# Groups of Q, K, V columns 512, 512, 352 and 352 wide in place of four of 432

## The chip, the cores and the metric

One core of a Trainium2 chip runs the program. The metric is the device time of one execution in microseconds (us). Three runs of the kernel before took 1100.6, 1100.63 and 1102.8 us; their median, 1100.63, is the time before.

The engines are TensorE (PE, with its weight loads PEld), VectorE (DVE), ScalarE (ACT), GpSimd (POOL) and SyncE (SP). DMAs are issued by SP, ACT and POOL. In a profile, ACTq and SPq are the sequencers of ACT and SP, on which a DMA issue or a wait takes time.

## The reference

One transformer block for 2048 tokens of 576 values, all float32: sliding attention (32 heads of 18, a window of 8 tokens at distance 2) and an FFN with squared relu run side by side on the same normalised input.

```python
xn = _layernorm(x, axis=-1)                      # S=2048, D=576
return x + _A_ref(xn, A_wqkv, A_wo) + _B_ref(xn, B_w1, B_b1, B_w2, B_b2)
...
qkv = (x @ wqkv).reshape(B, S, 3, H, Dh)         # H=32, Dh=18
idx = pos[:, None] - off[None, :]                # off = 0, 2, ..., 14
logits = einsum("bhsd,bhswd->bhsw", q, kg) * scale
attn = softmax(where(mask, logits, -1e9))
o = einsum("bhsw,bhswd->bhsd", attn, vg) @ wo
...
h = x @ w1 + b1                                  # F=4608
h = where(h > 0, h, 0) ** 2
out = h @ w2 + b2
```

## The kernel before, in words

**Tiles.** The tokens form four blocks of 512, each of four rows of 128 tokens. The 576 inputs are five chunks of 128 (the last holds the 64 left over, doubled). Every float32 operand is split into a high and a low part that TensorE takes: ACT copies the high part, DVE subtracts for the low one. A product is high·high, low·high and high·low, so a row of 128 tokens times one group of columns is 14 matmuls (`row_products`, L342).

**Groups.** The 32 heads form four groups of eight, 144 columns of each of Q, K and V. A group's K, V and Q columns lie side by side, 432 in all, and one matmul is 432 wide: one PSUM bank holds 512.

**Where these products are.** Group 0 of block 0 runs first, in the open rows (L1391 on, matmuls at L1472). Then come the plain rows of blocks 0 and 1 (`qkv_row`, L366): groups 1, 3, 2 of block 0, and 3, 2, 1, 0 of block 1, four rows each, in five PSUM banks by turns; the last two rows lie inside the first pair of FFN tiles. Blocks 2 and 3 are done later, two groups (0 and 1, then 2 and 3) and two blocks at a time, by a scheme with seven products in place of eight (`quad_step`, L1091, products at L1103 and L1107); its last two steps lie inside the second FFN phase.

**What follows a row.** ACT copies the PSUM bank into a staging slot (L358; in the quads L1113, where DVE may add a second bank) and one DMA writes the three 144-column parts to a scratch tensor in DRAM, `kvq[g]` (L360, L1117). ACT issues that DMA for plain rows; in the quads ACT, SP, or, for the last ones, GpSimd. Attention on DVE later loads K and V of a whole block with the tokens before it (1.3 MB each, L388) and Q (L386). `offer` puts an attention on the list once its group and block are stored.

**What sets the order.** The instructions of each engine are written out in order by hand, and each engine runs its own list strictly in that order. Every DMA of SP and ACT reports to one of eight counters (DMAHW0 to DMAHW7), handed out in turn over both engines in the order of the program; a DMA is issued only when the one eight earlier, the last on its counter, has landed, and its engine waits for that.

**What the steps touch.** L590 is an ACT copy to a high part for the left-over inputs, followed by DVE's subtraction at L118 (the helper `tt`, so all of DVE's subtractions bear L118). L323 and the next L118 split a group's weights. L515 and L118 split the first FFN weights into the slot `w1s`, which the FFN's first product reads (L677). L743 and L746 are the start of an FFN pair's second sum: one matmul, and ACT's copy of its bank into another, to which the product after it adds. L524 reloads split FFN weights, 1 MB each. L573 is the FFN's second matmul.

## Time and profile before

| | before |
|---|---|
| median of the runs | 1100.63 us |
| span of the profiled execution | 1098.5 us (its time is taken as the median's, 2.1 us more) |
| TensorE busy | 1092.3 us, 99% |
| VectorE busy | 879.9 us, 80% |
| ScalarE busy | 563.2 us, 51% |
| DMA moved | 298.97 MB, 272 GB/s on average |
| granted TensorE clock | 9 of tenths or more in all 40 slices |

Rows of the profile read as follows. A row of the timeline is start, length, engine, line, operation, what it writes <- what it reads, the shape, how many of them (x12), and in brackets the idle time of the engine before it, with what it is taken to have waited for. A row with three numbers behind the name of an operation gives the shortest, median and longest of its durations in ns. "DMA to landing" is the time from a DMA's issue to its last byte, again shortest, median and longest, in us. A row that begins with a window gives the busy time and the number of instructions of PE, PEld, DVE, ACT and POOL, then the granted clock, the DMA share and GB/s.

### The profile page before, as it was taken

Reading aid. Unit: us, or ns where it says so; the run is one execution under the profiler, and the core shown is the slowest. Engines: PE = TensorE matmul, PEld = TensorE weight load, DVE = VectorE, ACT = ScalarE, POOL = GpSimd, SP = SyncE. Lnnn points to the kernel's source line nnn. Section 1 sums busy time; section 2 is a strip of 40 time slices with the busy share of each in tenths; the row PEclk is TensorE's granted clock in tenths of the full one; section 3 lists DMA queues with packets and bytes.
Section 4 is the critical chain, followed back from the end, with each engine's and each line's share of the span. In section 5 each row is a group of like instructions: output and inputs, shape, how many; then the busy total and the mean of one; then the engine's idle time right before and its main releaser. Section 6 shows DMA issues by size and latency. Waiting matters only on the chain.

```text
span 1098.5 us, 13947 instructions
## 1 busy us (share of the span) xinstructions
PE 1092.3 (99%) x4936; PEld 922.9 (84%) x4936; DVE 879.9 (80%) x1183; ACT 563.2 (51%) x794; POOL 149.3 (14%) x267
## 2 busy tenths in 40 slices
PE   9999999999999999999999999999999999999998
PEld 7999888888888888888899988888888888888887
DVE  7687988899898979999879387776767676889955
ACT  5435666656666654555344345454554545543432
POOL 4000401031030101003010300201101010101010
PEclk9999999999999999999999999999999999999999
DMA  8966998879989887868565988868686877685582
GB/s 282 340 221 214 342 391 314 338 268 257 393 317 294 317 332 261 306 225 315 197 211 168 320 318 284 305 224 315 222 294 221 294 241 288 224 284 194 185 290 83
DMA packets 109558, 298.97 MB, mean 272 GB/s; under 512 B 12648, under 2 KB 42736, under 8 KB 98608
## 3 DMA queue, kind: packets, MB, share of 16 engines
q1 hardware_dynamic: 69984, 192.84, 50.1%
q0 software_dynamic: 13200, 62.52, 16.2%
q10 hardware_dynamic: 26304, 42.71, 11.7%
q8 instruction: 39, 0.64, 0.2%
q14 instruction: 31, 0.25, 0.1%
HBM read 213.53 MB, written 84.50 MB: 271 GB/s over the span
## 4 chain that ended last, share of the span: by engine, by line
PE 99%; DVE 0%; ACT 0%; issue 0%; POOL 0%; ACTq 0%; POOLq 0%
PE p L573 47%; PE p L677 35%; PE p L366 7%; PE p L1103 6%; PE p L1107 1%; PE p L1472 1%; PE p L683 1%; PE p L1389 0%; PE p L1434 0%; DVE w1s L118 0%; ACT X L122 0%; PE p L1371 0%; ACT h L723 0%; DVE w2s L118 0%; DVE r L118 0%
## 5 line engine op out<-in xcount | busy, mean ns | idle before, releaser
L573 PE MATMUL p<-h,w2s 128*128 128x512 f32 x2066 | 491.6, 389 | 0.2 <-ACT h L723 0.2
L573 PEld LDWEIGHTS p<-h,w2s 128*128 128x128 f32 x2066 | 387.5, 188 | 81.7 <-ACT h L723 0.6
L677 PE MATMUL p<-X,w1s 128*128 128x512 f32 x864 | 219.2, 389 | 0.0
L677 PEld LDWEIGHTS p<-X,w1s 128*128 128x128 f32 x864 | 162.2, 188 | 33.5
L546 ACT ACTIVATE w2s<-w2r 128x640 fp32r<-128x640 f32 x164 | 120.3, 735 | 128.1 <-PE p L573 98.3
L118 DVE TENSOR_TENSOR w2s<-w2r,w2s 128x576 fp32r<-128x576 f32 x164 | 123.5, 753 | 72.3 <-ACT w2s L546 70.7
L677 PE MATMUL p<-S,w1s 128*128 128x512 f32 x648 | 164.5, 389 | 0.0
L677 PEld LDWEIGHTS p<-S,w1s 128*128 128x128 f32 x648 | 121.6, 188 | 25.1
L444 POOL DMA_DIRECT2D o<-q x128 | 69.5, 609 | 418.2 <-DVE q L118 416.7
L719 ACT ACTIVATE r<-r,b1t 128x512 f32<-128x512 f32 x72 | 52.2, 725 | 116.8 <-DVE r L118 115.7
L415 DVE TENSOR_REDUCE lg<-pr 128x64 f32<-128x1152 f32 x64 | 86.5, 1351 | 1.2
L118 DVE TENSOR_TENSOR pr<-lg,kv 128x1152 f32<-128x1152 f32 x64 | 86.6, 1354 | 1.0
L118 DVE TENSOR_TENSOR pr<-q,kv 128x1152 f32<-128x1152 f32 x64 | 86.6, 1354 | 0.9
L118 DVE TENSOR_TENSOR pr<-pr 128x576 f32<-128x576 f32 (+1 forms) x128 | 77.6, 606 | 3.5
L118 DVE TENSOR_TENSOR r<-p,r 128x512 f32<-128x512 f32 (+1 forms) x77 | 53.1, 689 | 32.8 <-ACT r L785 15.3
L727 ACT ACTIVATE r<-r 128x1024 f32<-128x1024 f32 x72 | 76.1, 1056 | 1.2
L118 DVE TENSOR_TENSOR h<-r,h 128x1024 fp32r<-128x1024 f32 (+3 forms) x46 | 51.8, 1135 | 23.4 <-ACT r L727 14.9
L761 ACT ACTIVATE r<-p 128x512 f32<-128x512 f32 x36 | 21.5, 598 | 82.1 <-PE p L677 82.1
L118 DVE TENSOR_TENSOR w1s<-w1r,w1s 128x1024 fp32r<-128x1024 f32 (+2 forms) x42 | 46.2, 1103 | 9.5 <-ACT w1s L515 8.8
L719 ACT ACTIVATE r<-p,b1t 128x512 f32<-128x512 f32 x72 | 48.2, 671 | 0.3 <-PE p L683 0.2
L118 DVE TENSOR_TENSOR h<-h 128x1024 fp32r<-128x1024 f32 x36 | 43.9, 1220 | 2.9 <-ACT h L1000 2.8
L573 PE MATMUL p<-w1s,w2s 128*128 128x512 f32 x195 | 44.7, 389 | 0.0
(207 smaller groups left out, 1166.7 us busy)
## 6 DMA issues: line engine op xcount, KB each, us to landing
w2r<-in_w SPq DMA_DIRECT2D x144, 320.0 KB, 3.9
kv<-kvq POOLq DMA_DIRECT2D x30, 1296.0 KB, 8.6
w<-w1s SPq DMA_DIRECT2D x21, 1024.0 KB, 8.5
w1s<-w ACTq DMA_DIRECT2D x19, 1024.0 KB, 5.9
h<-r SPq DMA_DIRECT2D x36, 512.0 KB, 6.2
h<-h SPq DMA_DIRECT2D x36, 512.0 KB, 4.1
w<-w1s SPq DMA_DIRECT2D x15, 768.0 KB, 10.3
w1s<-w ACTq DMA_DIRECT2D x15, 768.0 KB, 5.1
```

Of the source, the lines that this page charges most:

```text
L118: return nc.vector.tensor_tensor(out=out, in0=a, in1=b, op=op)
L366: nc.tensor.matmul(p[:, :QW], l, r, start=k == 0, stop=k == len(mm) - 1)
L415: nc.vector.tensor_reduce(out=lg[:, j * HG:(j + 1) * HG].rearrange("p a w -> p w a"), in_=pr.rearrange("p w (a d) -> p w a d", d=DH), axis ...
L444: nc.gpsimd.dma_start(rows[:, i], q[i * L:(i + 1) * L, :, a:z])
L546: nc.scalar.activation(w2s[stream[i]][:, :DE], raw2[i], AF.Copy)
L573: nc.tensor.matmul(yp[b][c], v, a, start=c not in yb[b], stop=c in last and c not in [o[0] for o in ops[i + 1:]], skip_group_check=True)
L677: nc.tensor.matmul(to, l, r, start=start and i == 0, stop=i == len(mm) - 1, skip_group_check=True)
L683: nc.tensor.matmul(to, weight(LEFT, k, f), v, start=False, stop=k == 1, skip_group_check=True)
L719: nc.scalar.activation(to, a, AF.Relu, bias=b1t[:, f:f + 1])
L727: nc.scalar.activation(r, r, AF.Square)
L761: nc.scalar.activation(u[:, 0], bb, AF.Copy)
L1103: nc.tensor.matmul(to, l[:, js], r, start=start and n == 0, stop=n == len(mm) - 1, skip_group_check=True)
```

## The change

Each of groups 0 and 1 is made 512 wide: K, V and Q of its own, and 80 query columns of group 2 or 3. Groups 2 and 3 keep their K and V and the other 64 query columns: 352. The total of columns is the same.

A row now leaves in two DMAs in place of one. A wide row writes its three parts (3 × 144 columns) to its own scratch tensor and 80 columns to that of the group two further on; a narrow one writes 2 × 144 and 64. The staging slots grow to 512, so that the tile `st` holds three in place of four, and the tile `kv` five. The attention of a narrow group is offered only once its wide partner's rows are stored.

```diff
-QW = 3 * CG
+WIDE, NARROW = TB, 3 * CG - (TB - 3 * CG)
+MORE = WIDE - 3 * CG
+WIDTH = (WIDE, WIDE, NARROW, NARROW)
...
+    def cut(t, n, width=WIDE):
+        return [t[:, i * width:(i + 1) * width] for i in range(n)]
+
     def open_stage():
-        stage[0] = sb.tile([P, 2 * NS * P], F32, name="st")[:, :NJ * QW].rearrange("p (j c) -> p j c", c=QW)
+        stage[0] = cut(sb.tile([P, 2 * NS * P], F32, name="st"), 3)
...
-    def qkv_out(b, g, j, p, places=0):
-        st = stage[places][:, j]
-        nc.scalar.activation(st, p[:, :QW], AF.Copy)
-        to = kvq[g][:, PAD + b * TB:PAD + (b + 1) * TB].rearrange("i (p j) c -> p j i c", j=NJ)[:, j]
-        nc.scalar.dma_start(to, st.rearrange("p (i c) -> p i c", c=CG))
+    def store(queue, b, g, j, st):
+        n = 3 if WIDTH[g] == WIDE else 2
+
+        def rows(t):
+            return t[:, PAD + b * TB:PAD + (b + 1) * TB].rearrange("i (p j) c -> p j i c", j=NJ)[:, j]
+
+        queue.dma_start(rows(kvq[g])[:, :n], st[:, :n * CG].rearrange("p (i c) -> p i c", c=CG))
+        to = rows(kvq[g + 2])[:, 2, :MORE] if n == 3 else rows(kvq[g])[:, 2, MORE:]
+        queue.dma_start(to, st[:, n * CG:WIDTH[g]])
+
+    taken = [0]
+
+    def qkv_out(b, g, j, p):
+        places = stage[0] + stage.get(1, [])
+        st = places[taken[0] % len(places)]
+        taken[0] += 1
+        nc.scalar.activation(st[:, :WIDTH[g]], p[:, :WIDTH[g]], AF.Copy)
+        store(nc.scalar, b, g, j, st)
...
-            nc.tensor.matmul(p[:, :QW], l, r, start=k == 0, stop=k == len(mm) - 1)
-        qkv_out(b, g, j, p, places)
+            nc.tensor.matmul(p[:, :WIDTH[g]], l, r, start=k == 0, stop=k == len(mm) - 1)
+        qkv_out(b, g, j, p)
...
-            nc.scalar.activation(st, x, AF.Copy)
+            nc.scalar.activation(st[:, :width], x, AF.Copy)
             if y is not None:
-                tt(st, y, st, ALU.add)
-            to = kvq[gs[f]][:, PAD + n * TB:PAD + (n + 1) * TB].rearrange("i (p j) c -> p j i c", j=NJ)[:, j]
-            (nc.scalar if y is None else nc.gpsimd if "last" in stage else nc.sync).dma_start(to, st.rearrange("p (i c) -> p i c", c=CG))
+                tt(st[:, :width], y, st[:, :width], ALU.add)
+            store(nc.scalar if y is None else nc.gpsimd if "last" in stage else nc.sync, n, gs[f], j, st)
```

On TensorE and DVE the order of the instructions stays. ACT, SP and GpSimd get 48, 12 and 4 DMA issues more. This moves which DMA an issue waits for, since each takes a turn of the eight counters.

ACT before, the last three of the four rows of group 2 of block 0 (plain rows 9 to 11 of the program, counted from 1) and the copy L590:

```order
L358 ACTIVATE st<-p_665 128x432 [waits PE_49]
L360 DMA kvq_98<-st 128x3x144 [waits DMAHW7_49,Activation_49]
L358 ACTIVATE st<-p_684 128x432 [waits PE_49]
L360 DMA kvq_98<-st 128x3x144 [waits DMAHW0_49,Activation_49]
L358 ACTIVATE st<-p_706 128x432 [waits PE_49]
L360 DMA kvq_98<-st 128x3x144 [waits DMAHW1_49,Activation_49]
L590 ACTIVATE w1r<-w1r 128x896 [waits DMAHW3_49,DVE_49]
```

The same place of ACT in the changed kernel, where L590 is L610, L358 is L379, and a row's DMAs are L369 and L371:

```order
L379 ACTIVATE kv<-p_677 128x352 [waits PE_49]
L369 DMA kvq_98<-kv 128x2x144 [waits DMAHW3_49,Activation_49]
L371 DMA kvq_98<-kv 128x64 [waits DMAHW4_49]
L379 ACTIVATE st<-p_697 128x352 [waits PE_49]
L369 DMA kvq_98<-st 128x2x144 [waits DMAHW5_49,Activation_49]
L371 DMA kvq_98<-st 128x64 [waits DMAHW6_49]
L379 ACTIVATE st<-p_720 128x352 [waits PE_49]
L369 DMA kvq_98<-st 128x2x144 [waits DMAHW7_49,Activation_49]
L371 DMA kvq_98<-st 128x64 [waits DMAHW0_49]
L610 ACTIVATE w1r<-w1r 128x896 [waits DVE_49]
```

Ahead of L610 stand six DMA issues in place of three. The first row's second DMA waits for counter 4, the second row's for counter 6; the next fence shows what is on them.

SP before, the last two loads of a group's weights (L313) and the loads of Q, K and V for the first attention (L386, L388):

```order
L313 DMA r_609<-in_wqkv 128x864 [waits DMAHW7_49,DVE_49]
L313 DMA r_611<-in_wqkv 128x432 [waits DMAHW0_49,DVE_49]
L386 DMA q<-kvq_96 128x576 [waits DMAHW5_49,DMAHW1_49]
L388 DMA kv<-kvq_96 128x2592 [waits DMAHW2_49,DMASW0_49,Pool_49]
L388 DMA kv<-kvq_96 128x2592 [waits DMAHW3_49,DMASW1_49]
```

SP in the changed kernel, where they are L317, L406 and L408:

```order
L317 DMA r_619<-in_wide 128x1024 [waits DMAHW7_49,DMAHW6_49,DVE_49]
L317 DMA r_621<-in_wide 128x512 [waits DMAHW1_49,DVE_49]
L406 DMA q<-kvq_96 128x576 [waits DMAHW3_49]
L408 DMA kv<-kvq_96 128x2592 [waits DMAHW4_49,DMASW0_49,Pool_49]
L408 DMA kv<-kvq_96 128x2592 [waits DMAHW6_49,DMASW1_49]
```

K and V now sit on counters 4 and 6 in place of 2 and 3, and ACT's second DMAs of the two rows above come on these counters next. The load ahead of these three weight and Q loads (L317 `r_617`, on counter 4 as well) waits there for the second DMA of the third plain row.

ACT before at the start of the second FFN phase: rows of the last two quad steps (L1113, L1117), the copy L746, and a reload of FFN weights (L524):

```order
L1117 DMA kvq_98<-w1r 128x3x144 [waits DMAHW1_49,Activation_49]
L1113 ACTIVATE w1r<-p_4838 128x432 [waits PE_49]
L1113 ACTIVATE w1r<-p_4848 128x432 [waits PE_49]
L1117 DMA kvq_98<-w1r 128x3x144 [waits DMAHW4_49,Activation_49]
L1113 ACTIVATE w1r<-p_4849 128x432 [waits PE_49]
L1113 ACTIVATE st<-p_4838 128x432 [waits PE_49]
L1117 DMA kvq_98<-st 128x3x144 [waits DMAHW5_49,Activation_49]
L1113 ACTIVATE st<-p_4839 128x432 [waits PE_49]
L746 ACTIVATE p_5459<-p_5458 128x512 [waits PE_49]
L524 DMA w1s<-w_113 128x2048 [waits DMAHW6_49]
```

The same place in the changed kernel, where L1113 is L1134, L746 is L766 and L524 is L544:

```order
L369 DMA kvq_98<-w1r 128x2x144 [waits DMAHW0_49,Activation_49]
L371 DMA kvq_98<-w1r 128x64 [waits DMAHW2_49]
L1134 ACTIVATE st<-p_4870 128x352 [waits DMAHW3_49,PE_49]
L1134 ACTIVATE st<-p_4880 128x352 [waits DMAHW7_49,DMAHW1_49,PE_49]
L369 DMA kvq_98<-st 128x2x144 [waits DMAHW5_49,Activation_49]
L371 DMA kvq_98<-st 128x64 [waits DMAHW6_49]
L1134 ACTIVATE st<-p_4881 128x352 [waits DMAHW4_49,PE_49]
L1134 ACTIVATE w1r<-p_4870 128x352 [waits PE_49]
L369 DMA kvq_98<-w1r 128x2x144 [waits DMAHW7_49,Activation_49]
L371 DMA kvq_98<-w1r 128x64 [waits DMAHW0_49]
L1134 ACTIVATE w1r<-p_4871 128x352 [waits PE_49]
L766 ACTIVATE p_5521<-p_5520 128x512 [waits PE_49]
```

Ahead of L766 the last L371 waits for counter 0, which is that of the first L369 of this fence: eight DMAs, SP's among them, lie between the one and the other.

More of the change, by code (lines that the diff above doesn't have):

```diff
@@ L50, in block_kernel @@
 @with_exitstack
-def block_kernel(ctx: ExitStack, tc: tile.TileContext, x, xt, wqkv, wo, w1, b1, w2, b2, w1l, out):
+def block_kernel(ctx: ExitStack, tc: tile.TileContext, x, xt, wide, narrow, wo, w1, b1, w2, b2, w1l, out):
     nc = tc.nc
@@ L63, in block_kernel @@
     oe = out[DM:].rearrange("d (b t) -> b d t", b=NB)
+    wqkv = [wide[0], wide[1], narrow[0], narrow[1]]
     def kv_tile(n):
@@ L68, in block_kernel @@
     x0 = kv_tile(NJ * D).rearrange("p (j d) -> p j d", d=D)
-    w0 = sb.tile([P, NC - 1, QW], F32, name="w1r", bufs=2)
+    w0 = sb.tile([P, NC - 1, WIDE], F32, name="w1r", bufs=2)
     w4 = sb.tile([P, DE], F32, name="w2r", bufs=3)
-    r0 = [w0[:, c] for c in range(NC - 1)] + [w4[:, :QW]]
+    r0 = [w0[:, c] for c in range(NC - 1)] + [w4[:, :WIDE]]
     nc.scalar.dma_start(x0[:, 0, 288:], xv[0, :, 0, 288:])
     nc.sync.dma_start(x0[:, 0, :288], xv[0, :, 0, :288])
-    nc.scalar.dma_start(r0[0], wqkv[0, :, 0])
+    nc.scalar.dma_start(r0[0], wqkv[0][:, 0])
     nc.sync.dma_start(x0[:, 1], xv[0, :, 1])
@@ L311, in load_wq @@
             n = 2 if k < 2 else 1
-            r = raws[g, k] = sb.tile([P, 2, QW], F32, name="r4", bufs=4)[:, :n]
-            nc.sync.dma_start(r, wqkv[g, :, 2 * k:2 * k + n])
+            r = raws[g, k] = four()[:, :n, :WIDTH[g]]
+            nc.sync.dma_start(r, wqkv[g][:, 2 * k:2 * k + n])
     def open_wq(g, name):
@@ L319, in open_wq @@
             t = mt.tile([P, 2, 2, TB], F32R, name=tag, bufs=1 if name == "S" else 3)
-            wq[g, k] = t[:, :n, :, :QW]
+            wq[g, k] = t[:, :n, :, :WIDTH[g]]
     def wq_hi(g, k):
@@ L351, in row_products, with qkv_row @@
         return mm
+    def cut(t, n, width=WIDE):
+        return [t[:, i * width:(i + 1) * width] for i in range(n)]
     def open_stage():
-        stage[0] = sb.tile([P, 2 * NS * P], F32, name="st")[:, :NJ * QW].rearrange("p (j c) -> p j c", c=QW)
-    def qkv_out(b, g, j, p, places=0):
-        st = stage[places][:, j]
-        nc.scalar.activation(st, p[:, :QW], AF.Copy)
-        to = kvq[g][:, PAD + b * TB:PAD + (b + 1) * TB].rearrange("i (p j) c -> p j i c", j=NJ)[:, j]
-        nc.scalar.dma_start(to, st.rearrange("p (i c) -> p i c", c=CG))
-    def qkv_row(b, g, j, i, places):
+        stage[0] = cut(sb.tile([P, 2 * NS * P], F32, name="st"), 3)
[13 more added lines that the diff above has]
+        store(nc.scalar, b, g, j, st)
+    def qkv_row(b, g, j, i):
         p = bank(i)
@@ L1010, in load_half, with slot, split_slot @@
     def load_half(k, i):
-        t = raw[k, i] = sb.tile([P, 2, 2, QW], F32, name="w1r", bufs=2)
+        t = raw[k, i] = sb.tile([P, 2, 2, WIDTH[2 * k]], F32, name="w1r", bufs=2)
         for f in range(2):
-            nc.sync.dma_start(t[:, f], wqkv[2 * k + f, :, 2 * i:2 * i + 2])
+            nc.sync.dma_start(t[:, f], wqkv[2 * k + f][:, 2 * i:2 * i + 2])
     def load_sides(k):
-        t = raw[k, "left"] = sb.tile([P, 2, QW], F32, name="mb")
+        t = raw[k, "left"] = sb.tile([P, 2, WIDTH[2 * k]], F32, name="mb")
         for f in range(2):
-            nc.sync.dma_start(t[:, f], wqkv[2 * k + f, :, NC - 1])
-    def slot(name):
+            nc.sync.dma_start(t[:, f], wqkv[2 * k + f][:, NC - 1])
+    def slot(k, name):
+        width = WIDTH[2 * k]
         if name == B11:
-            ws[name] = [four(F32R)[:, :, :QW] for _ in range(2)]
+            ws[name] = [four(F32R)[:, :, :width] for _ in range(2)]
         else:
             t = mt.tile([P, 2, 2, TB], F32R, name="w1s" if name in (T1, T2, T3) else "h", bufs=3)
-            ws[name] = [t[:, i, :, :QW] for i in range(2)]
+            ws[name] = [t[:, i, :, :width] for i in range(2)]
         return ws[name]
-    def split_slot(name, v):
-        split(*slot(name), v)
+    def split_slot(k, name, v):
+        split(*slot(k, name), v)
     def split_side(k, f):
-        t = ws[LEFT, f] = four(F32R)[:, :, :QW]
+        t = ws[LEFT, f] = four(F32R)[:, :, :WIDTH[2 * k]]
         split(t[:, 0], t[:, 1], raw[k, "left"][:, f])
@@ L1057, in first_slots @@
         for name in (B11, T1, T2, T3):
-            slot(name)
+            slot(0, name)
         slot_hi(B11, v)
@@ L1079, in first_slots @@
         for f in range(2):
-            ws[LEFT, f] = four(F32R)[:, :, :QW]
+            ws[LEFT, f] = four(F32R)[:, :, :WIDE]
             soon(lambda f=f: nc.scalar.activation(ws[LEFT, f][:, 0], raw[0, "left"][:, f], AF.Copy))
@@ L1092, in quad_step @@
         b0, b1, gs = 2, 3, (2 * k, 2 * k + 1)
-        a, b, c, u = [bank(n)[:, :QW] if opened is None else opened for n, opened in
-                      zip((*QKV_BANKS[i], i), quad_banks[i])]
-        quad_banks[i] = [a, b, c, u]
+        width = WIDTH[2 * k]
+        quad_banks[i] = [bank(n) if opened is None else opened for n, opened in zip((*QKV_BANKS[i], i), quad_banks[i])]
+        a, b, c, u = [t[:, :width] for t in quad_banks[i]]
         js = slice(j * P, (j + 1) * P)
@@ L1109, in row @@
         def row(n, f, x, y=None):
-            places = stage[(rows_out[0] // NJ + 1) % 2]
-            st = places[:, rows_out[0] % NJ]
+            places = stage[1] + stage[0]
+            st = places[rows_out[0] % len(places)]
             rows_out[0] += 1
-            nc.scalar.activation(st, x, AF.Copy)
+            nc.scalar.activation(st[:, :width], x, AF.Copy)
             if y is not None:
-                tt(st, y, st, ALU.add)
-            to = kvq[gs[f]][:, PAD + n * TB:PAD + (n + 1) * TB].rearrange("i (p j) c -> p j i c", j=NJ)[:, j]
-            (nc.scalar if y is None else nc.gpsimd if "last" in stage else nc.sync).dma_start(to, st.rearrange("p (i c) -> p i c", c=CG))
+                tt(st[:, :width], y, st[:, :width], ALU.add)
+            store(nc.scalar if y is None else nc.gpsimd if "last" in stage else nc.sync, n, gs[f], j, st)
         ss = lambda n: lambda h, q: SS[n][:, h, q]
@@ L1175, in phase_b0 @@
                 load_left(b)
-                slot(B21)
+                slot(0, B21)
                 slot_hi(B21, raw[0, 1][:, 0])
@@ L1188, in phase_b0 @@
         kept_back[0] = 0
-        stage[1] = kv_tile(NJ * QW).rearrange("p (j c) -> p j c", c=QW)
+        stage[1] = cut(kv_tile(5 * WIDE), 5)
         def fourth_slot(k):
-            split_slot(T4, raw[k, 0][:, 0])
+            split_slot(k, T4, raw[k, 0][:, 0])
         def hook(k, half, s, i):
@@ L1201, in hook @@
             if at == (0, 0, 5, 0):
-                split_slot(B22, raw[0, 1][:, 1])
+                split_slot(0, B22, raw[0, 1][:, 1])
                 load_half(1, 1)
@@ L1206, in hook @@
                 if (s, i) == (1, 1):
-                    slot(B11)
+                    slot(1, B11)
                     slot_hi(B11, v)
@@ L1212, in hook @@
                     tt(v, w, v, ALU.subtract)
-                    slot(T1)
+                    slot(1, T1)
                     slot_hi(T1, v)
@@ L1220, in hook @@
                     tt(v, b22, v, ALU.subtract)
-                    slot(T2)
+                    slot(1, T2)
                     slot_hi(T2, v)
@@ L1225, in hook @@
                     tt(v, b21, v, ALU.subtract)
-                    slot(B21)
+                    slot(1, B21)
                     slot_hi(B21, b21)
                 if (s, i) == (4, 1):
-                    slot(T3)
+                    slot(1, T3)
                     slot_hi(T3, w)
@@ L1238, in hook @@
                     split_side(1, 1)
-                    split_slot(B22, b22)
+                    split_slot(1, B22, b22)
                     for g in (0, 1):
@@ L1243, in hook @@
                 if (s, i) == (3, 0):
-                    stage[1] = stage["last"] = sb.tile([P, NJ, QW], F32, name="w1r", bufs=2)
+                    stage[1] = cut(sb.tile([P, NJ * WIDE], F32, name="w1r", bufs=2), NJ)
+                    stage["last"] = True
                     kept_back[0] = 1
@@ L1376, in block_kernel @@
     for c in range(1, NC):
-        nc.sync.dma_start(r0[c], wqkv[0, :, c])
+        nc.sync.dma_start(r0[c], wqkv[0][:, c])
     for j in range(2, NJ):
@@ L1471, in part @@
             l = x4[0][:, js] if c == NC - 1 else X[0][:, 1 if a == 1 else 0, c, js]
-            nc.tensor.matmul(qp[j][:, :QW], l, (wlo if a == 2 else whi)(c), start=done[j] == 1, stop=done[j] == 3 * NC - 1)
+            nc.tensor.matmul(qp[j][:, :WIDE], l, (wlo if a == 2 else whi)(c), start=done[j] == 1, stop=done[j] == 3 * NC - 1)
         def parts(j, *which):
@@ L1558, in q0 @@
         pieces = [statistics(1), split_wq(3, "S")]
-        waiting = []
+        waiting, stored = [], {(0, 0)}
         def row(r):
@@ L1565, in row, with go @@
                 run(pieces, 1)
-            qkv_row(b, g, j, r % 5, r // NJ % 2 if r < 4 * NJ else 0)
+            if r == 4 * NJ:
+                stage.pop(1)
+            qkv_row(b, g, j, r % 5)
             if j == NJ - 1:
-                def go(b=b, g=g):
-                    offer(b, g)
-                if r < 6:
-                    waiting.append(go)
-                else:
-                    go()
+                stored.add((b, g))
+                ready = [g] if (b, (g + 2) % 4) in stored or g < 2 else []
+                if g < 2 and (b, g + 2) in stored:
+                    ready.append(g + 2)
+                for n in ready:
+                    def go(b=b, g=n):
+                        offer(b, g)
+                    if r < 6:
+                        waiting.append(go)
+                    else:
+                        go()
         for r in range(len(todo) - 2):
@@ L1579, in q0 @@
                 kept_back[0] = 0
-                stage[1] = kv_tile(NJ * QW).rearrange("p (j c) -> p j c", c=QW)
+                stage[1] = cut(kv_tile(5 * WIDE), 5)
+                taken[0] = 3
             row(r)
@@ L1658 @@
     q, k, v = rows(A_wqkv).reshape(NC, P, 3, D).transpose(2, 1, 0, 3)
-    wqkv = np.zeros((G, P, NC, QW), k.dtype)
-    for g in range(G):
-        own = slice(g * CG, (g + 1) * CG)
-        wqkv[g] = np.concatenate([k[:, :, own], v[:, :, own], q[:, :, own]], 2)
+    wide, narrow = [], []
+    for g in range(G // 2):
+        own, other = slice(g * CG, (g + 1) * CG), slice((g + 2) * CG, (g + 3) * CG)
+        wide.append(np.concatenate([k[:, :, own], v[:, :, own], q[:, :, own], q[:, :, other][:, :, :MORE]], 2))
+        narrow.append(np.concatenate([k[:, :, other], v[:, :, other], q[:, :, other][:, :, MORE:]], 2))
     wo = np.asarray(A_wo).reshape(G, CG, D)
@@ L1680 @@
         "xt": rows(xt).reshape(NC, P, NB, TB).transpose(2, 1, 0, 3),
-        "wqkv": wqkv,
+        "wide": np.stack(wide),
+        "narrow": np.stack(narrow),
         "wo": behind(wo),
```

## The prediction

> **What bounds the kernel now.** I read the page first: span, busy time, chain of work.

> ```profile
> span 1098.5 us, 13947 instructions
> PE 1092.3 (99%) x4936; PEld 922.9 (84%) x4936; DVE 879.9 (80%) x1183; ACT 563.2 (51%) x794; POOL 149.3 (14%) x267
> PE 99%; DVE 0%; ACT 0%; issue 0%; POOL 0%; ACTq 0%; POOLq 0%
> ```

> TensorE is busy for all but 6.2 of 1098.5 us, and the chain is TensorE from end to end. So only two things change the time: what the matmuls cost, and new waits of TensorE. The next view is the busy time by stretch, for the price of a matmul and for the places where another engine or the DMAs are nearly as late as TensorE.

> ```profile
> 200.00:400.00 200.00, 200.00 (x884) 165.68 (x883) 176.54 (x268) 122.77 (x166) 37.62 (x56) 1.00 0.91 314
> 20.74:92.13 71.39, 71.39 (x366) 68.52 (x366) 56.91 (x79) 31.03 (x53) 3.45 (x7) 1.00 0.77 257
> 54.00:80.00 26.00, 26.00 (x135) 25.00 (x134) 24.82 (x23) 7.57 (x12) 0.54 (x1) 1.00 0.64 203
> ```

> The columns are span, busy time of PE, weight loads, DVE, ACT, POOL, then granted clock (1.00), DMA share and GB/s. In the first stretch (200 to 400 us) all matmuls are 512 wide: 200/883 = 226.5 ns each. The second runs from the first plain row to the first FFN product; PE has no gap in it. In the third DVE is busy 24.82 of 26 us, so anything that makes DVE late there stays late.

> **The matmuls.** 848 matmuls change: 56 in the open rows, 392 in the plain rows, 400 in the quads; half become 512 wide, half 352.

> ```profile
> 31.81 2.51 PE L366 MATMUL p<-S,X 128*128 128x432 f32 x12
> 86.65 2.51 PE L366 MATMUL p<-h,X 128*128 128x432 f32 x12
> 1093.15 1.59 PE L1371 MATMUL p<-h,w2s 128*128 128x256 f32 x12
> L1371 PEld LDWEIGHTS p<-h,w2s x12: 187/192/192, 1092.9 to 1094.3; 128*128 128x128 f32 x12
> ```

> The first two rows lie 54.84 us and exactly 20 rows of 14 matmuls apart: 195.9 ns for one of 432. The third gives (1.59 − 0.283)/11 = 118.8 ns for 256, since the last one runs on for 283 ns. The line through 256 and 512 puts 432 at 192.8 and 352 at 159 to 160; 432 stands 3 ns above it. A pair of 512 and 352 so costs 386.6 ns against 391.7: −5 ns, and −2.1 to −6.1 if 352 also stands above the line or below it. Over 424 pairs that is **−2.0 us** (−0.9 to −2.6). A weight load of 190 ns as a floor for the 352 is ruled out by the same rows: the 256 go at 119 ns above such loads. [...]

> **First place: blocks 0 and 1, up to the first FFN product.** The stretch 20.74 to 92.13 holds 26 rows, in the order of groups 1, 3, 2, 3, 2, 1, 0: 10 become wide (+0.43 us each), 16 narrow (−0.50). The 56 open-row matmuls add 1.7 us before it, of which some 0.3 lies in their short waits. PE alone would arrive 1.4 + 4.3 − 8.0 = −2.4 us, at 89.8. But there it meets a chain through ACT and DVE:

> ```profile
> 51.21 0.53 ACT L358 ACTIVATE st<-p 128x432 f32<-128x432 f32 x1 [2.22 <-PE p L366]
> 51.77 0.37 ACTq L360 DMA_DIRECT2D kvq<-st  x1
> 52.24 0.95 ACT L590 ACTIVATE w1r<-w1r 128x896 fp32r<-128x896 f32 x1 [0.50 <-DMA kv<-kvq]
> 53.23 1.09 DVE L118 TENSOR_TENSOR w1r<-w1r 128x896 fp32r<-128x896 f32 x1 [3.29 <-ACT w1r L590]
> 82.92 2.54 DVE L118 TENSOR_TENSOR h<-r,h 128x864 fp32r<-128x864 f32 x3 [2.27 <-ACT h L323]
> 90.98 2.39 DVE L118 TENSOR_TENSOR w1s<-w1r,w1s 128x1024 fp32r<-128x1024 f32 x2
> 92.13 1.07 PE L677 MATMUL p<-X,w1s 128*128 128x512 f32 x4
> ```

> The row's copy and its store are issued on ACT, then L590, which DVE waits for (3.29 us idle); from then on DVE works through, and the first of its last two subtractions ends at about 92.2 (half of the 2.39 us). The third matmul at 92.58 (92.13 + 2 × 226.5 ns) reads it: 0.4 us of slack. So PE's 2.4 us gain ends in a wait here, and any delay of L590 beyond 0.4 us moves PE's arrival past today's.

> The change puts a second store behind each of the rows. With no wait it costs an issue of 0.37 us per row on ACT. PE ends the eleventh row 1.4 + 4 × 0.43 − 7 × 0.50 = −0.4 us from today, so L590 starts near 52.2 as now; the three wide subtractions at 82.92 (512 instead of 432 of each 1024) add 0.5, and the chain ends 0.1 us past its slack.

> But the two DMAs take two of eight completion counters that SP and ACT share in turn, and an issue waits on its own engine for the DMA eight earlier. The trace of before shows one such wait:

> ```profile
> L360 ACTq DMA_DIRECT2D kvq<-st x1: 366/366/366, 32.6 to 32.6; - x1
> DMA to landing us min/median/max: 8.3/8.3/8.3
> SPq L388 <- DMA kvq<-st: 1.3, 1, 1.3
> L388 SPq DMA_DIRECT2D kv<-kvq x2: 327/355/383, 41.0 to 41.4; - x2
> DMA to landing us min/median/max: 8.4/9.9/11.5
> 42.00:46.00 4.00, 4.00 (x22) 3.85 (x21) 3.93 (x5) 2.89 (x4) 0.13 (x1) 1.00 1.06 402
> 50.00:54.00 4.00, 4.00 (x22) 3.84 (x22) 0.77 (x1) 1.54 (x3) 0.00 (x0) 1.00 1.03 341
> ```

> A row's store went out at 32.6 and landed at 40.9; the K load, eight DMAs later, left SP at 41.0 after a wait of 1.3 us on it. K and V (1.3 MB each) landed at 49.4 and 52.9, with the DMA engines full (share 1.03 to 1.06). In the changed order K waits behind the first of three weight loads, which now waits for the second store of the third row (issued near 32.7, so landed near 41.0 by the 8.3 us): three loads, Q, K and V at about 0.4 us an issue put V at 43.6. By today's 11.5 us it lands at 55, by the 8.4 us at 52, and if the weight loads just ahead take their 1.3 MB at 0.4 MB/us it is 58; I take 55. The second store of the tenth row stands eight behind V, so ACT stops there until 55; then its issue, the eleventh row's copy, two issues (0.37 + 0.53 + 0.74 + 0.1) bring L590 to 56.8: **+4.6 us**. Queued behind it on DVE is the whole list from 53.23 to 92.2. With 0.5 for the wide subtractions and 0.4 of slack PE arrives at 92.13 + **4.7** (0.1 to 7.7). The two last wide rows of block 1, behind this point, add 28 × 30.6 ns = **+0.9**.

> **Blocks 2 and 3.** 400 matmuls give **−1.0 us** of the −2.0. DVE is not full in any quarter of the first pair of groups:

> ```profile
> 542.30:561.88 19.58, 19.58 (x101) 18.82 (x100) 17.07 (x26) 7.42 (x13) 0.00 (x0) 1.00 0.81 253
> 561.88:581.46 19.58, 19.58 (x101) 18.82 (x100) 14.78 (x16) 10.41 (x18) 5.41 (x10) 1.00 0.56 171
> ```

> Wide copies and subtractions there cost some 0.1 us each, one more issue a row 0.37; 2.5 us of slack cover them.

> **Second place: the start of the second FFN phase**, where the last two quad steps run inside it.

> ```profile
> L1117 ACTq DMA_DIRECT2D kvq<-w1r x1: 366/366/366, 610.4 to 610.4; - x1
> DMA to landing us min/median/max: 16.2/16.2/16.2
> 612.00:618.00 6.00, 6.00 (x32) 5.70 (x32) 1.21 (x2) 1.90 (x4) 1.47 (x3) 1.00 1.05 308
> 616.69 0.37 ACTq L1117 DMA_DIRECT2D kvq<-st  x1
> 619.28 0.58 ACT L746 ACTIVATE p<-p 128x512 f32<-128x512 f32 x1 [1.05 <-PE p L743]
> 622.01 1.30 PE L677 MATMUL p<-S,w1s 128*128 128x512 f32 x5
> ```

> The store of 610.4 took 16.2 us in a full DMA. In the changed order the second store of the third row from there waits for the first store of that row, and ACT's copy L746 stands behind it; the product at 622.01, near 621.3 with narrow rows, needs the copy. That store carries two thirds of the bytes: at a constant share it takes 10.8 us, else 16.2, from about 609.7. After it come an issue, a copy and L746 (1.5 us): L746 ends between 622.0 and 627.4, a stall of 0.7 to 6.1. I take 2.7, nearer to the row's two thirds.

> **At nothing:** the further edits, with the last rows' stores and those of block 1.

> ```profile
> L1117 POOL DMA_DIRECT2D kvq<-w1r x2: 769/777/785, 622.5 to 623.3; - x2
> DMA to landing us min/median/max: 2.1/2.2/7.4
> ```

> GpSimd issues four more stores of 0.78 us at 622 and later; attention, which they delay by 3.1 us, has nobody on TensorE waiting there. Twelve SP issues of 0.37 us lie in its idle time. Block 1's rows have three staging slots for four: their stores land in 2.2 us at the median (69 to 104 us), and three narrow rows take 3 × 14 × 0.16 = 6.7 us; behind the one of 7.4 us ACT's copy would wait 0.7 us, which TensorE's five banks cover. Later offers of the narrow groups leave DVE's order as it was.

> **Sum:** 4.7 + 0.9 − 1.0 + 2.7 = **+7.3 us**. The profiled execution is 1098.5 of span and by the shown median of 1100.6 some 2.1 around it: **1107.9 us**.

> **Rivals.**
> - *No lane binds.* If V lands before about 50.5 (its 8.4 us row speaks for it, the full DMA rows against), ACT meets no wait, and L746 has its copy in time: 0.2 + 0.9 − 1.0, **1100.7**, not slower. It decides at the tenth row's second store, with V there or not.
> - *Only the first place stalls:* 1100.6 + 4.6 = **1105.2**; for it, that narrow stores may free the counter at 610 early. Only the second: 1103.4.
> - *Both at their far ends:* 7.7 + 0.9 − 1.0 + 6.1, **1114.3**.
> - *The matmuls alone count* (DVE's list moves up with PE): **1098.6**. Against it stands the 0.4 us of slack.
> - *Short store rows.* The new second stores write runs of 320 and 256 bytes where all were 576; if these clog the full DMA, landings at both places get longer, and it ends like the far ends, 1114. [...]

> **How the numbers follow.** Forecast 0.42; first place only 0.20, second only 0.06; no lane 0.20; matmuls alone 0.04; far ends 0.08. Each spreads by about 1.5 us. About 0.2% (2.2 us) is what a measurement can tell from none. Within it fall "no lane" and part of "second only": same 0.23; the matmuls alone, at 1098.6, lie just inside the bound, half of them with a tail of "no lane" on the faster side: 0.06; slower 0.71. The range from 1099.8 to 1112.5 leaves out the matmuls alone, a quarter of no lane, and most of the far ends.

> **What would show it.** Right: ACT stops before a second store near 44 to 55 us, released by the V load; L590's successor starts near 57; PE idles some 4 us or more just ahead of the first FFN product; a gap of some 3 us at the product near 622; 352-wide matmuls at 160 ns. Wrong: ACT free at 50, PE's wait at the first product under 1 us, or 352-wide at over 165 ns.

## The result, and the profile after

The changed kernel takes 1119.8 us (median of 4 runs, 1117.9 to 1121.2) against 1100.7 for the kernel before: a ratio of 1.017 (95% interval 1.0156 to 1.0185). It is slower, as forecast, but by 19.2 us and not by 7.3, and outside the range. The page of the changed kernel begins so:

```profile
span 1117.5 us, 14021 instructions
PE 1098.1 (98%) x4936; PEld 913.5 (82%) x4936; DVE 879.8 (79%) x1183; ACT 562.6 (50%) x794; POOL 151.7 (14%) x271
PE 92%; DMA 3%; DVE 2%; ACT 1%; issue 1%; ACTq 1%; SPq 0%; POOL 0%; DVEq 0%; POOLq 0%
```

The count of matmuls is the same, but TensorE's chain is now broken: 8% of it goes through DMAs, DVE and ACT. Both traces hold the same 4936 matmuls in the same order, so the start of the n-th after, less its start before, tells where the time went (worked out from the two traces, us):

```
matmul no.   where                               before    after   difference
     120     third row of group 1, block 0         26.8     30.2      3.4
     280     blocks 0/1, narrow rows               58.1     57.6     -0.5
     480     behind the first FFN product          97.6    107.2      9.6
     560                                          115.9    126.4     10.6
    2440     before the quads                     542.1    552.8     10.8
    2640     quads, wide half done                581.3    598.2     16.9
    2820     quads, ahead of the second place     616.5    627.4     10.9
    2840     behind it                            620.8    639.6     18.7
    2900                                          634.0    653.2     19.2
    4930     end                                 1093.9   1113.1     19.2
```

Some 10.6 us come in at the first place and 8.3 at the second, with the quads near zero and nothing elsewhere. (In the quads the wide rows come first, so the difference rises there to 16.9 and the narrow rows take it back.)

**The matmuls.** Timeline of TensorE in the changed kernel, two narrow plain rows:

```profile
56.27 2.10 PE L386 MATMUL p<-S,X 128*128 128x352 f32 x12
58.53 2.10 PE L386 MATMUL p<-S,X 128*128 128x352 f32 x12
```

One row of 14 matmuls is 2.26 us: 161.4 ns each, where 159 to 160 was forecast.

**First place.** Timeline of ACT in the changed kernel, the second DMAs (L371) of the ninth and tenth plain row and the copy L610 (before: L590 at 52.24):

```profile
52.02 0.38 ACTq L369 DMA_DIRECT2D kvq<-kv  x1
54.18 0.33 ACTq L371 DMA_DIRECT2D kvq<-kv  x1
...
55.05 0.38 ACTq L369 DMA_DIRECT2D kvq<-st  x1
58.26 0.33 ACTq L371 DMA_DIRECT2D kvq<-st  x1
...
60.07 0.95 ACT L610 ACTIVATE w1r<-w1r 128x896 fp32r<-128x896 f32 x1 [0.97 <-ACT st L379]
```

The loads of K and V (L408), which stand eight DMAs ahead of these two, by the view of that line, and SP's timeline:

```profile
L408 SPq DMA_DIRECT2D kv<-kvq x2: 383/828/1273, 46.1 to 47.5; - x2
DMA to landing us min/median/max: 8.0/9.4/10.7
```

```profile
35.30 1.42 SPq L317 DMA_DIRECT2D r<-in_narrow  x3
36.82 0.37 SPq L217 DMA_DIRECT2D mb<-mr  x1
37.28 8.28 SPq L317 DMA_DIRECT2D r<-in_wide  x3
```

K landed at 46.14 + 8.0 = 54.1, and ACT's second DMA went at 54.18; V at 47.5 + 10.7 = 58.2, and the next went at 58.26. These two waits (1.8 and 2.8 us) are the ones forecast. But V left SP at 47.5 and not at 43.6. The three wide loads ahead of it took SP 8.28 us. SP's waits from 37 to 46 us (total, times, longest), the view of the fourth plain row's first store, and that of the third row's second one:

```profile
SPq L317 <- DMA kvq<-st: 2.8, 1, 2.8
SPq L317 <- DVE h L122: 2.6, 1, 2.6
```

```profile
L369 ACTq DMA_DIRECT2D kvq<-st x1: 407/407/407, 36.8 to 36.8; - x1
DMA to landing us min/median/max: 8.4/8.4/8.4
```

```profile
L371 ACTq DMA_DIRECT2D kvq<-st x1: 498/498/498, 34.0 to 34.0; - x1
DMA to landing us min/median/max: 2.0/2.0/2.0
```

The second of the three loads waited until 42.1 for DVE, which still read the buffer that it fills. The third waited until 45.2 for the store of the fourth row. K and V follow it. The third row's store, for which the forecast had them wait, had landed by 36.0.

From L610 on DVE works its list 7.8 us later than before. ACT's row copies stand behind work that waits for DVE, so TensorE's banks run full twice in block 1 (waits of 1.70 us at 71.7 and 1.50 at 82.6). Then TensorE waits for the weights of group 0, two rows ahead of the FFN's first product, and again at that product:

```profile
91.35 0.73 PE L386 MATMUL p<-h,X 128*128 128x512 f32 x2 [2.09 <-ACT h L327]
92.61 3.90 PE L386 MATMUL p<-h,X 128*128 128x512 f32 x10 [0.53 <-DVE h L122]
...
101.62 1.19 PE L697 MATMUL p<-X,w1s 128*128 128x512 f32 x4 [0.53 <-DVE w1s L122]
```

The third matmul of the FFN's first product starts at 101.62, where it was 92.58: 9.0 us later. The last two wide rows and small waits behind it make that 10.6. Note 3.90 us for ten matmuls at 92.61: more than 2.3.

**Second place.** Timeline of ACT, the view of the store at 622.5, and TensorE's timeline in the changed kernel:

```profile
622.53 0.38 ACTq L369 DMA_DIRECT2D kvq<-w1r  x1
...
630.05 0.38 ACTq L369 DMA_DIRECT2D kvq<-w1r  x1
635.37 0.33 ACTq L371 DMA_DIRECT2D kvq<-w1r  x1
635.74 0.46 ACT L1134 ACTIVATE w1r<-p 128x352 f32<-128x352 f32 x1 [7.83 <-DMA kvq<-w1r]
635.79 0.38 ACTq L544 DMA_DIRECT2D w1s<-w  x1
636.10 0.59 ACT L766 ACTIVATE p<-p 128x512 f32<-128x512 f32 x1
```

```profile
DMA to landing us min/median/max: 12.8/12.8/12.8
```

```profile
629.62 0.39 PE L763 MATMUL p<-X,w1s 128*128 128x512 f32 x1
636.26 2.92 PE L697 MATMUL p<-S,w1s 128*128 128x512 f32 x6 [6.24 <-ACT w1r L1134]
638.98 1.96 PE L1124 MATMUL p<-h,X 128*128 128x352 f32 x6
```

The same two products in the kernel before, without a wait between them:

```profile
618.86 0.39 PE L743 MATMUL p<-X,w1s 128*128 128x512 f32 x1
619.08 1.52 PE L677 MATMUL p<-S,w1s 128*128 128x512 f32 x6
```

The store of 622.53 landed 12.8 us later, at 635.3, and the DMA eight behind it, for which ACT stood, left at 635.37. TensorE waited 6.24 us, and not for L766: it waited for the row's copy ahead of it (L1134 at 635.74), which empties the PSUM bank that the next FFN product is summed in. Behind the wait six matmuls take 2.92 us. The view by stretch shows why, and that the same holds behind the first place:

```profile
92.00:96.40 4.40, 3.88 (x12) 3.03 (x12) 4.30 (x7) 2.26 (x5) 0.00 (x0) 0.61 0.40 118
636.00:641.50 5.50, 5.24 (x15) 4.67 (x16) 0.53 (x1) 0.69 (x2) 4.38 (x7) 0.50 1.02 419
```

The granted clock is 0.61 and 0.50 there. At half clock a 512-wide matmul takes 427 ns and a 352-wide one 293: 13 matmuls behind the second wait (five wide, eight narrow) lost 2.1 us by their pitch, five behind the first lost 1.0.

### The profile page after: what moved, and what is told of

Its sections match the earlier page's. It is cut to its first block, busy times and chain, and to the rows that moved or that the text cites. A ratio compares the mean times of both kernels' runs of the same rounds, so it can differ in the third digit from the quotient of the medians.

```text
span 1117.5 us, 14021 instructions
## 1 busy us (share of the span) xinstructions
PE 1098.1 (98%) x4936; PEld 913.5 (82%) x4936; DVE 879.8 (79%) x1183; ACT 562.6 (50%) x794; POOL 151.7 (14%) x271
## 3 DMA queue, kind: packets, MB, share of 16 engines
q0 software_dynamic: 13264, 62.36, 16.2%
## 4 chain that ended last, share of the span: by engine, by line
PE 92%; DMA 3%; DVE 2%; ACT 1%; issue 1%; ACTq 1%; SPq 0%; POOL 0%; DVEq 0%; POOLq 0%
PE p L593 46%; PE p L697 34%; PE p L1124 5%; PE p L386 2%; DMA kvq<-w1r 1%; DMA kvq<-st 1%; PE p L1128 1%; PE p L1493 1%; PE p L703 1%; DMA kv<-kvq 1%; ACT st L379 1%; ACTq L371 0%; PE p L1410 0%; DVE r L122 0%; DVE pr L122 0%
## 5 line engine op out<-in xcount | busy, mean ns | idle before, releaser
L697 PEld LDWEIGHTS p<-S,w1s 128*128 128x128 f32 x648 | 122.4, 189 | 32.6 <-ACT w1r L1134 6.7
L739 ACT ACTIVATE r<-r,b1t 128x512 f32<-128x512 f32 x72 | 52.2, 725 | 117.5 <-DVE r L122 117.3
L122 DVE TENSOR_TENSOR w1s<-w1r,w1s 128x1024 fp32r<-128x1024 f32 (+2 forms) x42 | 46.2, 1103 | 10.1 <-ACT w1s L535 9.4
L122 DVE TENSOR_TENSOR w1r<-w1r 128x256 f32<-128x256 f32 (+5 forms) x69 | 40.8, 591 | 8.2 <-ACT w1r L610 6.7
```

The source lines that it names most:

```text
L122: return nc.vector.tensor_tensor(out=out, in0=a, in1=b, op=op)
L697: nc.tensor.matmul(to, l, r, start=start and i == 0, stop=i == len(mm) - 1, skip_group_check=True)
L739: nc.scalar.activation(to, a, AF.Relu, bias=b1t[:, f:f + 1])
```

## The experiments

All ratios are to the kernel before, with 95% intervals. "Arrival" below is the difference of matmul 560 to its start in the kernel before: 10.6 in the changed kernel.

**Widths without the second DMA.** In `store`:

```diff
-        queue.dma_start(rows(kvq[g])[:, :n], st[:, :n * CG]...)
-        to = rows(kvq[g + 2])[:, 2, :MORE] if n == 3 else rows(kvq[g])[:, 2, MORE:]
-        queue.dma_start(to, st[:, n * CG:WIDTH[g]])
+        step = CG if n == 3 else (NARROW - CG) // 2
+        fr = bass.AP(tensor=st.tensor, offset=st.offset, ap=[st.ap[0], [step, 3], [1, CG]])
+        queue.dma_start(rows(kvq[g]), fr)
```

> The changed widths with one DMA a row in place of two: the second DMA is left out, and a narrow row's DMA writes three runs of 144 columns taken at a step of 104 from its 352, so that the last query columns are not what they should be (the 80 and 64 columns are not stored in their places). Counters (the second DMAs' waits on shared counters cost the time): the counters stand as in the kernel before, ACT's copy before the left-over split starts at 51.5 to 54 us, TensorE waits under 1 us ahead of the first FFN product and under 0.5 us at the copy of the second phase; 1099 to 1102.5 us. Widths (the lateness of the four wide rows and the longer splits alone push the loads of K and V back): the copy still starts after 56 us and the time stays above 1106.

Measured: 1102.4 us, ratio 1.0028 (1.0009 to 1.0048). ACT's timeline, and TensorE's ahead of the first FFN product:

```profile
51.60 0.95 ACT L610 ACTIVATE w1r<-w1r 128x896 fp32r<-128x896 f32 x1 [0.44 <-DVE w1r L122]
```

```profile
90.08 0.73 PE L697 MATMUL p<-X,w1s 128*128 128x512 f32 x2
92.08 1.20 PE L697 MATMUL p<-X,w1s 128*128 128x512 f32 x4 [1.27 <-DVE w1s L122]
```

L610 is at 51.6, TensorE arrives at 90.1 and waits for `w1s` until 92.1: the "no lane" rival as it was described, down to the third matmul, and 0.28% slower than before where it was priced at no change. With one DMA a row 17 of the 19 us are gone. The wait was 1.3 us where under 1 was expected. The runs spread more than those of the kernel before: seven of ten took 1101.2 to 1103.4 us, three 1107.1 to 1109.3. In the profiled run (1103.4) the arrival is only 0.5; most of the rest is one wait of 1.96 us at 358.5 for a load (`mb`), which most other traces don't have.

**The kernel before with two DMAs a row** (2 × 144 and 144 columns, all of 576-byte runs):

```diff
-        nc.scalar.dma_start(to, st.rearrange("p (i c) -> p i c", c=CG))
+        fr = st.rearrange("p (i c) -> p i c", c=CG)
+        for i in (slice(0, 2), slice(2, 3)):
+            nc.scalar.dma_start(to[:, i], fr[:, i])
```

(and the same in `quad_step`.)

> The kernel before, 432 wide, with each row stored by two DMAs (2 x 144 and 144 columns). Counters: the same DMAs wait for each other as in the changed kernel, so both waits come back: a gap of 3 to 8 us ahead of the first FFN product, and one of 3 to 7 us at the second product of the second phase, each followed by a stretch at half the granted clock; 1111 to 1121 us. Widths: nothing but 0.37 us an issue, hidden; 1100 to 1103 us.

Measured: 1113.7 us, ratio 1.0122 (1.0105 to 1.0139). ACT and TensorE:

```profile
52.68 2.67 ACTq L362 DMA_DIRECT2D kvq<-st  x2
...
56.90 0.95 ACT L592 ACTIVATE w1r<-w1r 128x896 fp32r<-128x896 f32 x1 [0.97 <-ACT st L358]
```

```profile
96.50 0.75 PE L679 MATMUL p<-X,w1s 128*128 128x512 f32 x2 [1.92 <-ACT w1s L517]
...
630.43 1.66 PE L679 MATMUL p<-S,w1s 128*128 128x512 f32 x6 [2.13 <-ACT st L1115]
...
639.43 2.62 PE L679 MATMUL p<-S,w1s 128*128 128x512 f32 x6 [2.85 <-ACT r L763]
```

Both places come back at the old width: the doubling of the DMAs alone costs some 13 us. So the short rows of 320 and 256 bytes aren't needed for that much. The gap ahead of the first product was smaller (1.9) than the 3 to 8 expected, since TensorE is not early here. At the second place the wait came as two, 2.1 and 2.9 us, where one of 3 to 7 was expected, and only the second was followed by half clock (a granted clock of 0.54 from 639.50 to 643.00 us, and of 1.00 from 630.00 to 634.00). The profiled run (1116.4) is the slowest of the four.

**Second DMAs off the counters.** They are issued by GpSimd, first for groups 3 and 2 of block 0, then for the last rows of the quads too:

```diff
-        queue.dma_start(to, st[:, n * CG:WIDTH[g]])
+        (nc.gpsimd if b == 0 and g > 1 else queue).dma_start(to, st[:, n * CG:WIDTH[g]])
```

> The changed kernel with the second DMAs of eight rows (groups 3 and 2 of block 0) issued by GpSimd, whose DMAs use no counter of SP and ACT; same bytes, same short runs. Counters: ACT's copy (L610 in the changed kernel) starts at 52 to 55 us, the waits ahead of the first FFN product fall from 9 to 1 to 3 us, the second place stays; 1110 to 1113 us. Short runs or bytes (the DMAs are late because of what the second stores write): the copy stays after 58 us; 1118 to 1121.

Measured: 1114.2 us, ratio 1.0127 (1.0112 to 1.0142); arrival 4.2, and the second place as in the changed kernel. L610 starts at 53.7, where the counters had put it. The eight rows account for 6.4 us; the total was forecast to fall further by 1 to 4 us. The move takes the issue time of these DMAs off ACT as well as their waits, so this run alone doesn't tell the two apart.

> As pool_first, and the second DMAs of the four last rows of the quads that ACT issued also go to GpSimd. Counters: the wait of ACT for the store of 622 goes, ACT's copy L766 ends in time, TensorE's gap of 6.2 us and the half clock behind it go; 1101 to 1104 us. Short runs or bytes: the gap stays over 4 us; 1109 or more if the first place is mended, else 1118.

Measured: 1114.6 us, ratio 1.0127 (1.0112 to 1.0142): a miss. The old gap went (the product after L763 waits no more), but a new one of 6.0 us came 44 matmuls later. ACT's timeline:

```profile
638.05 0.46 ACT L1134 ACTIVATE w1r<-p 128x352 f32<-128x352 f32 x1 [9.29 <-DMA kvq<-w1r]
```

This is the eighth of the last rows. It waits for a store from its staging slot: 4 slots of 512 in `w1r` and 3 in `st` are seven places for eight rows, where there were eight.

**Eight slots for the last rows:** pool_both with

```diff
-                    stage[1] = cut(sb.tile([P, NJ * WIDE], F32, name="w1r", bufs=2), NJ)
+                    stage[1] = cut(sb.tile([P, NJ * WIDE], F32, name="w1r", bufs=2), 5, NARROW)
```

> pool_both with eight staging slots for the last eight rows in place of seven (the tile w1r cut into five of 352 in place of four of 512). Slots (the gap of 6.2 us at 639 us in pool_both comes from ACT's copy of the eighth row, which waits until the first row's late second store has left its slot): gap under 1 us there and no half clock behind it; 1103 to 1107 us. Rival (it is the full DMA that makes the reloads of FFN weights late, whatever the slots): the gap stays over 4 us; 1111 or more.

Measured: 1108.6 us, ratio 1.0071 (1.0057 to 1.0086), 6 us under pool_both, 1.6 above what was expected: gaps of 1.3 us each remain at 638 and 678.

> one_store (one DMA a row; the last query columns of each row are not stored in their places) with eight slots for the last eight rows: only the widths are left of the change. Slots: the gap of 0.9 us at 631 us goes; 1100.5 to 1102, under one_store by 0.5 to 1.5. If widths alone gain what the matmuls do (2 us): 1098 to 1099. If widths alone cost (the chain ahead of the first product, the late loads): 1101 or more.

Measured: 1103.3 us, ratio 1.0031 (1.0016 to 1.0046), no different from one_store. The gap at 631 went, but smaller ones came at 647 and 672. So the widths by themselves gain nothing here: by the two intervals the bare change costs 0.1 to 0.5%. Again three of the runs (of twelve) took 1108 us or more.

**What is left at the first place.** First the same eight slots with more on GpSimd (all of block 0 but the open rows):

> The same with the second DMAs of the first four plain rows (group 1 of block 0) on GpSimd as well. Counters (in pool_both the first four rows' second DMAs still hold back ACT, and behind it SP's loads: V leaves at 48.1 us, 42.5 in one_store): V leaves before 45, the wait ahead of the first FFN product falls by 3 to 4 us against pool_both; 1100 to 1104 us, and under pool_both_slots by 2 to 4. Rival (GpSimd's own work on the second statistics is delayed instead, or the short runs are what is slow): V still after 46.5, the same time as pool_both_slots within 1 us.

Measured: 1109.4 us, ratio 1.0078 (1.0065 to 1.0091); V left at 46.1, between the two forecasts, and the arrival got worse, 6.5 against 4.8. The time is within 1 us of pool_both_slots, as the rival had it. ACT's timeline has the place:

```profile
33.78 0.79 ACT L327 ACTIVATE S<-r 128x704 fp32r<-128x704 f32 x1 [2.35 <-DMA r<-in_narrow]
```

The weights of group 3 land 1.5 us later than in pool_both_slots (L327 there at 32.22). They left SP no later (27.3 against 27.4) and took 6.4 us in place of 4.4. Why wasn't found out.

Then the second DMAs of the four open rows, and of the four rows after them, on SP, with the same turns of the counters:

```diff
+        (nc.sync if (b, g) == (0, 0) else nc.gpsimd if ... else queue).dma_start(to, ...)   # open_on_sp
+        (nc.sync if b == 0 and g < 2 else nc.gpsimd if ... else queue).dma_start(to, ...)   # open_on_sp2
```

> pool_both_slots with the second DMAs of the four open rows (group 0 of block 0) issued by SP, which is idle there; they keep their turns of the counters. ACT's time (each second DMA takes 0.55 us of ACT, which is the late engine in the open rows): ACT's last copy of the open rows (L1574) starts at 23 to 24 us in place of 25.5, the arrival at the first FFN product falls by 1.5 to 2.5 us, 1106 to 1107.3 us. Rival (the counters or the DMAs are what is late there): L1574 after 25, time within 0.7 us of pool_both_slots (1108.6).

Measured: 1107.2 us, ratio 1.0057 (1.004 to 1.0073). ACT's last copy of the open rows, in pool_both_slots and here:

```profile
25.34 0.79 ACT L1574 ACTIVATE xf<-p 128x128 f32<-128x128 f32 x4 [0.99 <-ACT st L379]
```

```profile
23.78 0.79 ACT L1574 ACTIVATE xf<-p 128x128 f32<-128x128 f32 x4 [0.50 <-ACT st L379]
```

1.6 us earlier with nothing changed but the engine that issues four DMAs, yet only 0.8 of it reached the arrival (4.0), where 1.5 to 2.5 was expected.

> The same with the second DMAs of the first four plain rows (group 1 of block 0) on SP as well. ACT's time: another 0.5 to 1.5 us off, 1104.8 to 1107 us. Rival (SP stands behind these second DMAs, each of which waits for a row's copy, and its loads get later): equal to open_on_sp or slower by up to 2 us.

Measured: 1104.8 us, ratio 1.0039 (1.0024 to 1.0054), arrival 2.3. It does the whole of the reference's work and is the fastest full version of the change; it is still slower than the kernel before.

**K and V off the counters.** The changed kernel with the first Q, K and V loads on GpSimd (`lane[0] = nc.gpsimd` moved ahead of `offer(0, 0)`):

> The changed kernel with the first Q, K and V loads issued by GpSimd, so that they take no turn of SP's and ACT's counters; every row's two DMAs stay on ACT. Counters (ACT's second DMAs of the ninth and tenth row wait for K and V): these two waits of 1.8 and 2.8 us go, L610 starts at 54.5 to 57 us in place of 60.1, the arrival at the first FFN product falls by 3 to 6 us; 1114 to 1117 us. Rival (only ACT's issue time counts, the waits would be there for the row stores anyway): L610 after 59, 1118.5 or more.

Measured: 1119.5 us, ratio 1.0167 (1.0148 to 1.0186): a miss. No DMA of ACT waits for K or V any more, but ACT's timeline has another wait; below it the view of the loads of K and V on GpSimd:

```profile
44.59 0.33 ACTq L371 DMA_DIRECT2D kvq<-st  x1
44.96 0.46 ACT L379 ACTIVATE kv<-p 128x352 f32<-128x352 f32 x1 [7.12 <-DMA kvq<-st]
```

```profile
L408 POOL DMA_DIRECT2D kv<-kvq x2: 527/530/532, 32.6 to 33.1; - x2
```

The second DMA of the fourth row now waits from 38.3 to 44.6 for the third row's store on the same counter. That store left at 34.6, 1.0 us later than in the changed kernel, and took 10.0 us to land in place of 2.2. K and V had just left, at 32.6 and 33.1 in place of 46.1 and 47.5, since they no longer stand behind SP's waits. With their 2.6 MB the DMA share from 34 to 36 us is 1.17, where it was 0.46. So the edit does more than free the counters: it also puts the two long loads ahead of the stores. L610 starts at 60.5. The run doesn't separate the theories.

> open_on_sp2 with the first Q, K and V loads on GpSimd. No wait of ACT is left on them in open_on_sp2 ahead of L610, so little should come of it: 1103.5 to 1105.5 us. If it falls below 1102, the rest of the loss was in those loads after all.

Measured: 1105.1 us, ratio 1.0039 (1.0026 to 1.0052), as expected.

**The half clock.** The changed kernel, with the one matmul ahead of the second wait issued 28 times:

```diff
-        if first:
+        for _ in range((28 if s else 1) if first else 0):
             nc.tensor.matmul(bb, weight(B11, 0, 0), A11(0, 0), start=True, stop=True, skip_group_check=True)
```

> The changed kernel with the one matmul that opens a bank ahead of the wait at 630 us issued 28 times in place of once (6.1 us of work that changes nothing in the result), so that TensorE works in most of that wait. Clock (TensorE runs at half clock after it has stood still): the 13 matmuls at 427 ns behind the wait go at 226.5, 2.0 to 2.6 us off, 1116.5 to 1118.5 us. Rival (the matmuls behind the wait are slow because of what they read, or the DMAs): no change, 1118.5 to 1121, and half clock as before.

Measured: 1117.6 us, ratio 1.0154 (1.0141 to 1.0167). TensorE's timeline and the stretch behind the wait:

```profile
629.28 6.51 PE L763 MATMUL p<-X,w1s 128*128 128x512 f32 x28
636.92 1.66 PE L697 MATMUL p<-S,w1s 128*128 128x512 f32 x6 [1.14 <-ACT w1r L1134]
```

```profile
636.00:641.50 5.50, 4.58 (x23) 4.07 (x24) 0.52 (x1) 1.42 (x3) 3.82 (x6) 1.00 1.01 417
```

The wait for ACT is still there, filled with idle work, and the granted clock is 1.00 where it was 0.50: some 2 us come back for 6 us of useless matmuls.

## Why the prediction was wrong, step by step

- **What bounds the kernel, and where the change hurts:** right. TensorE has no time to spare, the gain of the matmuls ends in a wait, and both new waits are near where they were put.
- **Matmuls, −2.0 us:** right, within its range. A pair now costs 226.7 + 161.4 ns against 391.7: −3.6 ns, −1.5 us over 424 pairs. The difference never reached the end of the program.
- **First place, +4.7 and +0.9:** the mechanism was right (ACT held by K and V, L610 late, DVE's list behind it), the size wrong: 10.6. The step that failed is "three loads, Q, K and V at about 0.4 us an issue put V at 43.6". It has the loads wait for the third row's store, "landed near 41.0 by the 8.3 us", but the 8.3 us are those of the fourth row's store. The third row's took 2.3 us before (of 30.36), its second one 2.0 here, and none of the three loads waited for it. That the loads were held past 41 all the same, by DVE until 42.1, is luck. V left SP 3.9 us later than forecast, mostly because the third weight load waits for the store of the *fourth* row (36.81, landed 8.4 us later; a wait of 2.8), a counter wait that was in the order and not priced; K's own issue took 1.3 us. So V landed at 58.2 and not at 55, and L610 came at 60.07 and not at 56.8. From there to the FFN's third matmul the delay grew by 1.2 us, where 0.1 was charged; the last wide rows cost 0.9 as forecast, small waits at 121 and 123 us 0.6.
- **Second issues on ACT,** "With no wait it costs an issue of 0.37 us per row on ACT": wrong too. In the open rows ACT is itself late, and a second issue takes it 0.5 us; SP's loads stand behind ACT's results there. open_on_sp2 against pool_both_slots gives 2.5 us for the first eight rows' second issues. pool_first puts 6.4 us on the second DMAs of the next eight rows; L610 moves by as much there (60.07 to 53.69), and 4.6 of it are the two waits seen on ACT. The half clock behind 92 us adds little to that: TensorE loses 1.0 us by it and then waits 1.3 us less for `w1s` than in pool_first (0.20 against 1.52).
- **Quads, −1.0:** about −0.4 by the matmuls' shifts (19.2 less 10.8 at the first place and 8.8 at the second); a loss of 0.3 us at 609.5 took some of it.
- **Second place, +2.7:** mechanism right (the counter, the very DMA, 12.8 us between the ends of 10.8 and 16.2), size wrong: 6.4 of wait and 2.4 of slow clock. With 12.8 us the forecast's own sum gives the 2.7 that it took, so the store's time isn't what failed. The step that failed is "the product at 622.01, near 621.3 with narrow rows, needs the copy": the wait is for the row's copy just ahead of L746, which frees a PSUM bank for the product at 619.08, so TensorE asks some 2 us earlier than the 621.3. And the store left some 2 us later than "from about 609.7" (622.53 less the 10.8 of the first place is 611.7), since the wide rows come first in the quads. Nothing was charged for the half clock.
- **At nothing:** the staging slots were weighed for block 1 only. In the quads seven slots for eight rows cost nothing while the counters were later still, and 6 us once they weren't. "TensorE's five banks cover" didn't hold in block 1 (3.2 us of waits), but these waits only came ahead of one for the same late list of DVE.
- **Rivals:** *matmuls alone* fell with one_store; *short store rows* aren't needed for 13 of the 19 us, by before_two_stores, and whether they have a part in the rest wasn't tested; *both at their far ends* came nearest and was still 5.5 us too cheap; *no lane* was the right picture of what remains without the second DMA, 2 us too cheap.

What stays open: why the weights of group 3 land later in pool_more_slots, and what would remove the rest in the best version, 0.4% above the kernel before: 2.3 of the 4.4 us in its trace are still at the first place, the others small waits behind 630 us.

## What to carry to other kernels

## What the runs showed of the hardware

In the changed kernel the granted clock was 0.50 from 636.00 to 641.50 us, behind a wait of 6.24 us, and 0.61 on average from 92.00 to 96.40 us, behind two waits of 2.09 and 0.53 us within 1.3 us. With the longer wait filled with matmuls (busy_wait) it was 1.00 from 636.00 to 641.50 us.

The clock records of the traces show more. In the changed kernel 0.50 holds from 92.08 to 95.49 and from 634.80 to 641.62 us, 3.41 us and twice that; in the kernel before it is 1.00 from 6.62 to 1098.88 us. Cut the trace of the changed kernel into steps of 3.41 us that begin at these switches. Two steps at full clock have TensorE standing still for 2.09 us (88.66 to 92.08) and 3.41 us (631.38 to 634.80), and each is followed by half clock; the next longest, 1.63 us (68.18 to 71.60) and 1.37 us (627.97 to 631.38), are not. In before_two_stores waits of 1.92 and 0.51 us, ahead of 96.50 and 97.76, were followed by a clock of 0.51 from 98.40 to 104.00, and one of 2.13 us ahead of 630.43 was followed by 1.00 from 630.00 to 634.00. What decides between such waits isn't shown.
